# First MoE, layer one, as seven products over pairs of token blocks, with x operands streamed from DRAM

## The chip, the cores and the metric

The kernel runs on one core of one Trainium2 chip. The metric is device time in microseconds (us), from the start to the end of one execution. TensorE is PE in the profile, VectorE DVE, ScalarE ACT, GpSimd POOL; SP issues the DMAs.

## The reference, cut to what matters

Attention with pooled queries gives x (2304 tokens x 512). A first mixture of experts (MoE) with 8 experts follows, then a second, soft one. The change concerns the first:

```python
P = sinkhorn_like(x @ w_gate)                 # 2304 x 8
for e in range(8):
    h = np.maximum(x @ w1[e], 0.0)            # layer one: 2304x512 @ 512x1024
    out += P[:, e:e + 1] * (h @ w2[e])        # layer two: 2304x1024 @ 1024x512
```

## The kernel before

Every float32 product is made from three matmuls in the shorter type fp32r: each operand is held as a high half (ACT copies it) and a low half (DVE subtracts the high half from the original), and PE adds hi·hi, hi·lo and lo·hi in one PSUM bank. So each operand costs an ACT and a DVE operation, called a split below; its halves stand side by side in one tile.

The tokens form 9 blocks of 256. The names: `xa` is the output of attention, `xs` an x tile with both halves, `w` a tile of W1, `v` of W2, `g` a PSUM bank of layer one, `hr` the rectified result, `ht` a sum of quarters of h, `ho` a split of h, `y` a PSUM bank of layer two, `acc` the output's accumulator.

Attention comes first: score matmuls (L189), their maximum on DVE (L190), exponentials on ACT (L221), sums of these on POOL (L225, L227). It takes a table of hooks: work for the MoE that is put between its steps (one split of w, one of x, four loads).

Then follow the experts. For experts 0 to 6 `period(e, i, after)` writes one block's work in a fixed text order: the seven products (L583) of layer two of block i, mixed with four quarters (`g1`, L541 to L549) of layer one of the next block. Layer one of a quarter is 24 matmuls of 128x256 (4 rows of D by 2 columns of F by 3), 96 per block and 864 per expert. Layer two of these experts is already done in seven products over halves of tokens, F and D (`PRODUCTS`): `h_sum` makes s1 to s4 on DVE, `h_split` splits seven operands, each product is 12 matmuls, and an eighth is never made. `v_sum` and `v_split` do this for W2. Expert 7 has an order of its own, since the tail of the kernel is woven into it.

The order on each engine is that of the text: the tile framework gives waits but moves nothing. Around the products the text is filled up by `slot()` (the gate's steps and the first preparations) and by `at(name, ...)` (splits of the next expert's weights). x of all blocks is stored to DRAM once (`xd`, 1 MB a block with both halves) and loaded again for each block of every expert (`load_x`, three buffers). The last phase loads the second MoE's weights (`load_m2`) as buffers come free. All these DMAs are on SP's queue.

Of the kernel before, what the change touches and what calls it, by code (L numbers as in the profile page):

```python
# [8 lines left out]
F32 = mybir.dt.float32  # L9
# [348 lines left out]
def tile_attention__moe__softmoe(ctx, tc, q, k, v, w_gate, w1, w2, phi, m2_w1, m2_w2, out):  # L358
# [9 lines left out]
    stg_p = ctx.enter_context(tc.tile_pool(name="stg", bufs=4))  # L368
# [49 lines left out]
    ]  # L418

    def stage(e, p):  # L420
        t = stg_p.tile([128, 1024], F32, tag="stg", name="stg")
        if isinstance(p, tuple):
            src = w2[e][512 * p[0]:512 * p[0] + 512, 256 * p[1]:256 * p[1] + 256].rearrange("(c p) d -> p c d", p=128)
            nc.sync.dma_start(out=t.rearrange("p (c d) -> p c d", c=4), in_=src)
        elif p < 4:
            src = w1[e][:, 256 * p:256 * p + 256].rearrange("(k p) f -> p k f", p=128)
            nc.sync.dma_start(out=t.rearrange("p (k f) -> p k f", k=4), in_=src)
        else:
            src = w2[e][256 * (p - 4):256 * (p - 4) + 256].rearrange("(c p) d -> p c d", p=128)
            nc.sync.dma_start(out=t.rearrange("p (c d) -> p c d", c=2), in_=src)  # L430
        staged[e, p] = t

    def split_w(e, p, eng=None):
        t = staged.pop((e, p))
        if p > 3:
            u = wpools["m"].tile([128, 2, 1024], F32R, tag="v", name="v", bufs=7)
        elif (4 * e + p) % 5 == 0:
            u = wp_p.tile([128, 2, 1024], F32R, tag="wp", name="w", bufs=1)
        else:
            u = wpools["m"].tile([128, 2, 1024], F32R, tag="w", name="w", bufs=4)  # L440
        nc.scalar.copy(u[:, 0], t)
        (eng or nc.vector).tensor_tensor(out=u[:, 1], in0=t, in1=u[:, 0].bitcast(F32), op=ALU.subtract)  # L442
        pieces[e, p] = u

    V = {}


    def v_sum(e, k):
        q = [staged[e, x] for x in ((0, 0), (0, 1), (1, 0), (1, 1))]
        if k == 4 and e == 0:  # L450
            staged[e, "t4"] = stg_p.tile([128, 1024], F32, tag="stg", name="t4")
        elif k == 4:
            staged[e, "t4"] = q[2]
        dst, a, b = {1: (q[0], q[1], q[0]), 2: (q[0], q[3], q[0]), 3: (q[1], q[3], q[1]), 4: (staged.get((e, "t4")), q[2], q[0])}[k]
        nc.vector.tensor_tensor(out=dst, in0=a, in1=b, op=ALU.subtract)

    def v_split(e, j):
        src = staged[e, ((0, 0), (1, 0), (0, 0), (0, 0), (0, 1), (1, 1), "t4")[j]]
        u = V[e, j] = wpools["m"].tile([128, 2, 1024], F32R, tag="v", name="v", bufs=7)
        nc.scalar.copy(u[:, 0], src)  # L460
        nc.vector.tensor_tensor(out=u[:, 1], in0=src, in1=u[:, 0].bitcast(F32), op=ALU.subtract)


    X, Hh, acc, Xd = {}, {}, {}, {}

    def x_tile(v):
        pool, tag = (wpools["m"], "x") if v % 3 else (wp_p, "x0")
        X[v] = pool.tile([128, 2, 4, 256], F32R, tag=tag, name="xs", bufs=2 if v % 3 else 1)
        return X[v]

    def split_x(i):
        u = x_tile(i)
        src = xa[i].rearrange("p k n -> p (k n)")
        hi, lo = (u[:, z].rearrange("p k n -> p (k n)") for z in range(2))
        nc.scalar.copy(hi, src)
        nc.vector.tensor_tensor(out=lo, in0=src, in1=hi.bitcast(F32), op=ALU.subtract)
        if i:
            store_x(i)
# [35 lines left out]

    Ho = {}
# [4 lines left out]
    def h_sum(i, name):  # L520
# [7 lines left out]
        nc.vector.tensor_tensor(out=o, in0=a, in1=b, op=op)  # L528

    def h_split(i, j):  # L530
        x = PRODUCTS[j][0]
        src = Ho[i, x] if isinstance(x, str) else part(i, *x)
        o = Ho[i, j] = m_p.tile([128, 2, 4, 128], F32R, tag="ho", name="ho", bufs=4)
        nc.scalar.copy(o[:, 0], src)  # L534
        nc.vector.tensor_tensor(out=o[:, 1], in0=src, in1=o[:, 0].bitcast(F32), op=ALU.subtract)  # L535

    def g1(e, i, fp, mid=None):
        x = X[NBLK * e + i]  # L540
# [636 lines left out]
```

## Time and profile before

| | |
|---|---|
| median of 3 runs | 2209.32 us (2208.95 to 2210.77) |
| span of the profiled execution | 2207.6 us |
| PE busy | 2162.6 us (98%) |
| DVE busy | 1280.8 us (58%) |
| ACT busy | 852.7 us (39%) |
| POOL busy | 414.5 us (19%) |

The median is of other executions than the profiled one; 1.7 us lie between it and the span. Busy shares are averages over three stages: attention up to about 530 us, the first MoE with experts 0 to 6 and then expert 7, and the end. POOL works in attention alone.

### The profile page before, as it was taken

What the parts mean: (1) busy time and instruction counts of PE and PEld (TensorE: products, weight loads), DVE (VectorE), ACT (ScalarE), POOL (GpSimd) and SP (SyncE); (2) the same over time, 40 slices, a digit from 0 to 9 for tenths busy, and PEclk for the clock granted to TensorE, in tenths of its full rate; (3) what the DMA queues carried; (4) which work ended last, traced back from release to release, by engine and by line L of the source; (5) the groups of instructions that cost most, each with busy time, mean ns of one, the idle gap of its engine ahead of it and who ended that gap; (6) DMA issues with size and microseconds to landing.
All of it is one profiled execution on the core that took longest, in us unless ns stands there. A gap on an engine that the chain in (4) does not pass through costs nothing.

```text
span 2207.6 us, 40414 instructions
## 1 busy us (share of the span) xinstructions
PE 2162.6 (98%) x16789; PEld 1955.1 (89%) x16789; DVE 1280.8 (58%) x2391; ACT 852.7 (39%) x1779; POOL 414.5 (19%) x305
## 2 busy tenths in 40 slices
PE   7999999998999999999999999999999999999997
PEld 5777777766999999999999999999999999999863
DVE  5777777775565654665474456447445744633451
ACT  3555555554433432333243233324233432311232
POOL 5888878874000000000000000000000000000000
PEclk9999999999999999999999999999999999999998
DMA  7554565451122221212122121212112121566668
GB/s 171 142 119 114 129 137 122 108 152 45 58 77 87 77 87 39 96 58 77 58 87 85 41 96 59 77 49 96 67 59 87 68 77 49 186 257 221 224 228 277
DMA packets 125045, 239.66 MB, mean 109 GB/s; under 512 B 44096, under 2 KB 95808, under 8 KB 110144
## 3 DMA queue, kind: packets, MB, share of 16 engines
q1 hardware_dynamic: 124864, 237.08, 34.8%
q8 instruction: 133, 2.18, 0.4%
q14 instruction: 48, 0.39, 0.1%
HBM read 189.87 MB, written 14.16 MB: 92 GB/s over the span
## 4 chain that ended last, share of the span: by engine, by line
PE 95%; DVE 2%; DMA 1%; ACT 1%; POOL 1%; issue 0%; SPq 0%; ACTq 0%; DVEq 0%; POOLq 0%
PE y L583 29%; PE g L547 13%; PE g L549 12%; PE g L548 12%; PE se L218 7%; PE o L234 7%; PE S L189 4%; PE y L659 2%; PE y L660 1%; PE y L661 1%; PE f L1075 1%; DMA kd<-kp 1%; PE t L133 1%; PE t L244 1%; PE t L109 1%; PE t L202 1%
## 5 line engine op out<-in xcount | busy, mean ns | idle before, releaser
L583 PE MATMUL y<-v,ho 128*128 128x256 f32 x5292 | 678.1, 283 | 4.0 <-DVE ho L535 2.2
L583 PEld LDWEIGHTS y<-v,ho 128*128 128x128 f32 x5292 | 654.0, 192 | 4.3 <-DVE ho L535 2.4
L547 PE MATMUL g<-xs,w 128*128 128x256 f32 x2304 | 654.9, 284 | 0.0
L549 PE MATMUL g<-xs,w 128*128 128x256 f32 x2304 | 652.0, 283 | 1.0 <-DVE w L442 1.0
L548 PE MATMUL g<-xs,w 128*128 128x256 f32 x2304 | 651.9, 283 | 0.0
L547 PEld LDWEIGHTS g<-xs,w 128*128 128x128 f32 x2304 | 441.9, 192 | 5.4 <-issue 4.0
L548 PEld LDWEIGHTS g<-xs,w 128*128 128x128 f32 x2304 | 442.1, 192 | 1.0
L549 PEld LDWEIGHTS g<-xs,w 128*128 128x128 f32 x2304 | 442.0, 192 | 1.2 <-DVE w L442 1.2
L565 ACT ACTIVATE hr<-g 128x512 f32<-128x512 f32 x252 | 150.5, 597 | 731.1 <-PE g L549 729.2
L595 DVE SCALAR_TENSOR_TENSOR acc<-y,P,acc 128x256 f32<-128x256 f32 x378 | 181.0, 481 | 321.0 <-PE y L583 321.0
L227 POOL TENSOR_TENSOR acc<-acc,e 128x576 f32<-128x576 f32 x224 | 319.0, 1424 | 64.7 <-ACT e L221 54.5
L190 DVE TENSOR_REDUCE m<-S 128x1 f32<-128x384 f32 x432 | 230.5, 547 | 86.7 <-PE S L189 75.1
L763 POOL MEMSET HT<- 128x1024 f32 x2 | 1.9, 960 | 1385.9 <-ACT ho L534 1375.0
L221 ACT ACTIVATE e<-se 128x288 f32<-128x288 f32 x576 | 206.7, 411 | 88.1 <-PE se L218 84.9
L218 PE MATMUL se<-q,kd 128*128 128x288 f32 x1152 | 223.4, 311 | 2.1 <-ACT e L221 0.3
L218 PEld LDWEIGHTS se<-q,kd 128*128 128x128 f32 x1152 | 178.0, 190 | 17.0 <-ACT e L221 9.8
L528 DVE TENSOR_TENSOR ht<-hr 128x512 f32<-128x512 f32 x126 | 86.7, 688 | 177.8 <-ACT hr L565 177.7
L534 ACT CAST ho<-ht 128x512 fp32r<-128x512 f32 x252 | 149.8, 618 | 85.6 <-DVE ht L528 71.1
L234 PE MATMUL o<-e,vr 128*64 128x288 f32 x1152 | 171.5, 419 | 0.0
L535 DVE TENSOR_TENSOR ho<-ht,ho 128x512 fp32r<-128x512 f32 x252 | 166.7, 681 | 4.0 <-ACT ho L534 3.5
L189 PE MATMUL S<-kd,q 128*128 128x384 f32 x384 | 146.2, 385 | 5.1 <-DVE m L190 3.1
L535 DVE TENSOR_TENSOR ho<-hr,ho 128x512 fp32r<-128x512 f32 x189 | 129.6, 686 | 17.5 <-ACT ho L534 17.5
(170 smaller groups left out, 1793.0 us busy)
## 6 DMA issues: line engine op xcount, KB each, us to landing
xs<-xd SPq DMA_DIRECT2D x90, 1024.0 KB, 4.8
stg<-in_moe_w_dram SPq DMA_DIRECT2D x60, 512.0 KB, 5.7
kd<-kp SPq DMA_DIRECT2D x32, 576.0 KB, 6.4
m2w<-in_moe_w_dram SPq DMA_DIRECT2D x13, 1024.0 KB, 7.0
m2w<-in_moe_w_dram SPq DMA_DIRECT2D x24, 512.0 KB, 8.8
kr<-in_k_dram SPq DMA_DIRECT2D x32, 288.0 KB, 7.0
qr<-in_q_dram SPq DMA_DIRECT2D x16, 576.0 KB, 3.7
kd<-kp SPq DMA_DIRECT2D x32, 288.0 KB, 3.6
```

The costliest lines, as they stand in the source:

```text
L189: nc.tensor.matmul(ps, lhsT=w, rhs=r[:, 384 * n:384 * n + 384], start=True, stop=True)
L190: nc.vector.tensor_reduce(out=M_[ph][:, x, n:n + 1], in_=ps, axis=AX.X, op=ALU.max)
L218: nc.tensor.matmul(ps, lhsT=kd[:, z, 128 * c:128 * c + 128], rhs=y[:, h, g], start=z == 0, stop=z == 1)
L221: nc.scalar.activation(out=e[:, g], in_=ps, func=AF.Exp, scale=1.0 / 16)
L227: nc.gpsimd.tensor_tensor(out=acc_[ph], in0=acc_[ph], in1=e, op=ALU.add)
L234: nc.tensor.matmul(O_[ph][64 * g:64 * g + 64, :288], lhsT=raws["v"][pi][:, h, c, :], rhs=E_[ph, c][:, g], start=c == 0, stop=c == 8,)
L535: nc.vector.tensor_tensor(out=o[:, 1], in0=src, in1=o[:, 0].bitcast(F32), op=ALU.subtract)
L547: nc.tensor.matmul(o, lhsT=w[:, 0, kk, c], rhs=x[:, 0, kk], start=kk == 0, stop=False)
L548: nc.tensor.matmul(o, lhsT=w[:, 0, kk, c], rhs=x[:, 1, kk], start=False, stop=False)
L549: nc.tensor.matmul(o, lhsT=w[:, 1, kk, c], rhs=x[:, 0, kk], start=False, stop=kk == 3)
L583: nc.tensor.matmul(ps, lhsT=o[:, x, c], rhs=v[:, w, c], start=first and c + z == 0, stop=c + z == 5, skip_group_check=not first,)
L595: nc.vector.scalar_tensor_tensor(out=y, in0=ps, scalar=p, in1=y, op0=ALU.mult, op1=ALU.add)
```

## The change

Layer one of experts 0 to 6 is made in seven products too. The blocks are taken in four pairs (u = 0 to 3) and one single block (u = 4), in the order 0, 1, 4, 2, 3. D and F are halved, W1 is four quarters (11, 12, 21, 22), and the two blocks of a pair are the two columns of a 2x2 product. W1 is needed in seven forms: 11, 12, 22 and the sums S1 to S4. x is needed in seven operands per pair: B11, B21 and B22 (halves of blocks) and the sums T1 to T4. A `chunk(e, u, n, c)` is 12 matmuls: product n, half c of the 512 columns of F. A pair has 14 chunks, so 168 matmuls where two blocks had 192; the single block keeps 8 chunks, 96 matmuls.

Each operand of x is split once, 35 in all, stored in DRAM as 512 KB and loaded for every expert into three buffers. Preparing them is the larger part of what moves: the operands of two pairs and half of a third, three W1 sums with their splits and a fourth sum, and the four W2 sums (stored raw in DRAM) are now hooks in attention; 15 more steps are spread over expert 0. The sums of the next expert's weights, and s3 and s4 of h, go to POOL.

The result of product 0 (shared by four outputs) is copied by ACT into two PSUM banks, `seed0` and `seed1`, into which products 2, 3 and 4 then accumulate; ACT copies or rectifies what stands there between them. Products 5 and 6 stand in `g` banks and are added on DVE into `hr`. PSUM now has two `g` banks (before 3) and three of tag m (before 2), two of which are the seeds during these experts.

The core of the diff:

```diff
+    PAIR = [("11", "B11"), ("12", "B21"), ("S2", "T2"), ("S3", "T3"), ("22", "T4"), ("S1", "T1"), ("S4", "B22")]
+    ONE = [("11", "B11"), ("12", "B21"), ("S1", "B11"), ("22", "BD")]
...
+    def x_split(u, op, part):
+        t = stg_p.tile([128, 2, 512], F32R, tag="stg", name="xt")
+        nc.scalar.copy(t[:, 0], part)
+        nc.vector.tensor_tensor(out=t[:, 1], in0=part, in1=t[:, 0].bitcast(F32), op=ALU.subtract)
+        Xd[u, op] = dram_p.tile([128, 1024], F32, name=f"xd{u}{op}")
...
+    def load_x(n=1):
+        for _ in range(n):
+            if xseq:
+                key = xseq.pop(0)
+                t = Xt[key] = wp_p.tile([128, 2, 2, 256], F32R, tag="x", name="xs", bufs=3)
+                nc.sync.dma_start(out=t.rearrange("p z k n -> p (z k n)").bitcast(F32), in_=Xd[key[1:]])
...
+    for h, step, fs in ((-210, 8, prep(0)), (-134, 4, prep(1)), (-36, 8, X2[:4])):
+        for n, f in enumerate(fs):
+            hooks[h + step * n] = [f]
+            hooks[h + step * n + 2] = [store_x]
...
+        -92: lambda: w_split(0, "11"),
+        -88: lambda: w_sum(0, "S3"),
+        -80: lambda: w_split(0, "S3"),
+        -72: lambda: w_sum(0, "S1"),
+        -64: lambda: w_sum(0, "S2"),
+        -56: lambda: w_split(0, "S2"),
+        -48: lambda: w_split(0, "12"),
+        -40: lambda: w_sum(0, "S4"),
+        -24: lambda: load_x(3),
...
+        -276: lambda: v_store(1),
+        -266: lambda: v_store(3),
+        -256: lambda: v_store(2),
+        -246: lambda: v_store(4),
...
-    pg = ctx.enter_context(tc.tile_pool(name="pg", bufs=3, space=PSUM, reuse_waits="tile"))
+    pg = ctx.enter_context(tc.tile_pool(name="pg", bufs=2, space=PSUM, reuse_waits="tile"))
+    pm = ctx.enter_context(tc.tile_pool(name="pm", bufs=3, space=PSUM, reuse_waits="tile"))
...
+    def chunk(e, u, n, c):
+        one = u == 4
+        form, op = (ONE if one else PAIR)[n]
+        first = n in ((0, 2) if one else (0, 5))
+        if first:
+            G[c] = pg.tile([128, 512], F32, tag="g", name="g")
+        mid = not one and n in (2, 3, 4)
+        ps = seed[c] if mid else G[c]
...
+        if c == 1:
+            if one:
+                load_x((0, 0, 2, 1)[n])
+            else:
+                load_x()
...
+        elif n in (2, 3):
+            nc.scalar.copy(quad(B, n - 2, c, True), ps)
+        elif n == 4:
+            relu(quad(A, 1, c, True), ps)
         else:
...
+            o = quad(B, 6 - n, c)
+            nc.vector.tensor_tensor(out=o, in0=ps, in1=o, op=ALU.add)
+            relu(o, o)
...
+                    pos = merge(e, u, ch, "cppcppcppcpcccc", (pe_, i))
...
+            merge(e, u, ch, "cccccc", None)
+            r = bounds[e, u] = len(items) - 1
+            pos = merge(e, u, ch, "pccppcppcpp", (e, 2 * u))
...
+            for form, d in (("S3", -6), ("S1", -4), ("S2", 1), ("S4", 5)):
+                at(r + d, (w_sum, n, form, nc.gpsimd), **late)
...
+            for k, d in ((1, 16), (3, 18), (2, 23), (4, 25)):
+                at(r + d, (v_sum, n, k, nc.gpsimd), **late)
...
+    for j, f in enumerate([*prep(4), *X2[4:], *prep(3)]):
+        at(starts[0, 1] + 2 + 3 * j, (f,), **late)
+        at(starts[0, 1] + 4 + 3 * j, (store_x,), **late)
```

In the texts given to `merge`, c is a chunk and p a product of layer two.

PE, in a steady pair of the changed kernel: six chunks stand in a row on the seed banks, then products (L706) and chunks in `g` banks are mixed. A row with x12 is a chunk or a product.

```order
L706 MATMUL y_10278<-v_9476,ho_10357 128x256 x12
L661 MATMUL seed0_6742<-xs_10229,w_9071 128x256 x12
L661 MATMUL seed1_6760<-xs_10229,w_9071 128x256 x12
L661 MATMUL seed0_6742<-xs_10272,w_8809 128x256 x12
L661 MATMUL seed1_6760<-xs_10272,w_8809 128x256 x12
L661 MATMUL seed0_6742<-xs_10354,w_8855 128x256 x12
L661 MATMUL seed1_6760<-xs_10354,w_8855 128x256 x12
L706 MATMUL y_10505<-v_9114,ho_10471 128x256 x12
L661 MATMUL g_10533<-xs_10439,w_8941 128x256 x12
L661 MATMUL g_10548<-xs_10439,w_8941 128x256 x12
L706 MATMUL y_10565<-v_9196,ho_10527 128x256 x12
```

Before, a run of 24 single matmuls of L547 to L549 on one `g` bank stood between two products; the rows below are the first and the last ones around one such run.

```order
L583 MATMUL y_13752<-v_13280,ho_13659 128x256 x12
L583 MATMUL y_13639<-v_13446,ho_13705 128x256 x12
L547 MATMUL g_13785<-xs_13134,w_13077 128x256
L548 MATMUL g_13785<-xs_13134,w_13077 128x256
L549 MATMUL g_13785<-xs_13134,w_13077 128x256
```

What moved: chunks are half as long, take another x tile each time, and product 1 comes three pieces after the last seed chunk.

SP's queue behind the single block of an expert in the changed kernel; `xd4` is the single block's operand, `xd2` those of the next pair, PE_49 a wait for PE, DMAHW for the landing of an earlier DMA.

```order
L565 DMA xs_12091<-xd4BD_7333 128x1024 [waits DMAHW3_49,PE_49]
L565 DMA xs_12323<-xd2B11_5999 128x1024 [waits DMAHW5_49,PE_49]
L565 DMA xs_12325<-xd2B21_6177 128x1024 [waits DMAHW4_49,PE_49]
L565 DMA xs_12356<-xd2T2_7528 128x1024 [waits DMAHW6_49,PE_49]
L565 DMA xs_12397<-xd2T3_7392 128x1024 [waits DMAHW7_49,PE_49]
```

And PE there: the third form reads xs_11936, whose buffer the load of xs_12323 takes.

```order
L661 MATMUL g_12297<-xs_11936,w_11083 128x256 x12
L661 MATMUL g_12310<-xs_11936,w_11083 128x256 x12
L661 MATMUL g_12297<-xs_12091,w_11009 128x256 x12
L661 MATMUL g_12310<-xs_12091,w_11009 128x256 x12
L661 MATMUL g_12359<-xs_12323,w_10853 128x256 x12
```

Before, one load of a whole block stood on SP's queue for each block, three blocks ahead of its use:

```order
L486 DMA xs_11496<-xd4_7369 128x2048
L427 DMA stg_11618<-in_moe_w1_dram 128x4x256
L486 DMA xs_11732<-xd5_7634 128x2048
L427 DMA stg_11851<-in_moe_w1_dram 128x4x256
L486 DMA xs_11965<-xd6_7899 128x2048
```

What moved: a load now waits for a tile that PE releases two chunks before the loaded tile is used.

POOL at the change from one expert to the next, in the changed kernel: W1 sums (L452), W2 sums (L483) and s3, s4 of h (L628). Before, POOL's last row ahead of the tail was a sum of attention (L227), so nothing stood here, and these sums were DVE's.

```order
L452 TENSOR_TENSOR stg_10721<-stg_10721,stg_10717 128x1024
L628 TENSOR_TENSOR ht_11185<-hr_10897 128x512
L628 TENSOR_TENSOR ht_11187<-hr_10930,ht_11183 128x512
L483 TENSOR_TENSOR stg_10916<-stg_11065,stg_10916 128x1024
L483 TENSOR_TENSOR stg_11065<-stg_11121,stg_11065 128x1024
L483 TENSOR_TENSOR stg_10916<-stg_11121,stg_10916 128x1024
```

What moved: eight sums of 128x1024 per change of expert and two of 128x512 per block went from DVE to POOL.

## Rows read from the trace of the kernel before

**Rows 1.** The page: busy time of each engine, and the chain that ended last.
```profile
PE 2162.6 (98%) x16789; PEld 1955.1 (89%) x16789; DVE 1280.8 (58%) x2391; ACT 852.7 (39%) x1779; POOL 414.5 (19%) x305
...
PE 95%; DVE 2%; DMA 1%; ACT 1%; POOL 1%; issue 0%; SPq 0%; ACTq 0%; DVEq 0%; POOLq 0%
```

**Rows 2.** Windows: length, busy PE, PEld, DVE, ACT, POOL (count), clock, DMA share, GB/s.
```profile
200.00:400.00 200.00, 198.94 (x1321) 141.93 (x1321) 150.83 (x325) 115.25 (x312) 161.97 (x116) 1.00 0.53 122
540.00:550.00 10.00, 6.03 (x47) 5.19 (x46) 6.79 (x10) 4.37 (x7) 0.00 (x0) 0.93 0.25 105
550.00:560.00 10.00, 10.00 (x82) 8.53 (x82) 8.58 (x13) 6.62 (x11) 0.00 (x0) 0.90 0.11 41
1000.00:1200.00 200.00, 200.00 (x1669) 200.00 (x1669) 109.22 (x181) 69.38 (x113) 0.00 (x0) 1.00 0.20 69
2100.00:2207.00 107.00, 86.84 (x772) 52.45 (x771) 41.31 (x123) 29.88 (x100) 0.00 (x0) 0.92 0.81 261
```

**Rows 3.** Timeline of ACT in attention: start, length, engine, line, operation.
```profile
403.89 1.45 ACT L221 ACTIVATE e<-se 128x288 f32<-128x288 f32 x4
...
435.02 1.45 ACT L221 ACTIVATE e<-se 128x288 f32<-128x288 f32 x4
...
468.27 1.45 ACT L221 ACTIVATE e<-se 128x288 f32<-128x288 f32 x4
```

**Rows 4.** Timeline of DVE in attention: the two low halves of the hooks.
```profile
447.04 1.33 DVE L442 TENSOR_TENSOR w<-stg,w 128x1024 fp32r<-128x1024 f32 x1
...
461.93 1.70 DVE L476 TENSOR_TENSOR xs<-x,xs 128x1024 fp32r<-128x1024 f32 x1 [0.25 <-ACT xs L475]
```

**Rows 5.** Groups by form, 800 to 1800 us: busy, mean ns | idle before, releaser.
```profile
L595 DVE SCALAR_TENSOR_TENSOR acc<-y,P,acc 128x256 f32<-128x256 f32 x325 | 155.6, 481 | 276.6 <-PE y L583 276.6
L535 DVE TENSOR_TENSOR ho<-ht,ho 128x512 fp32r<-128x512 f32 x188 | 124.3, 681 | 0.0
L534 ACT CAST ho<-ht 128x512 fp32r<-128x512 f32 x188 | 111.5, 617 | 70.5 <-DVE ht L528 58.4 <-PE y L583 12.1
L565 ACT ACTIVATE hr<-g 128x512 f32<-128x512 f32 x185 | 110.5, 597 | 567.1 <-PE g L549 567.1
L528 DVE TENSOR_TENSOR ht<-hr 128x512 f32<-128x512 f32 x93 | 64.0, 688 | 132.6 <-ACT hr L565 132.6
L461 DVE TENSOR_TENSOR v<-stg,v 128x1024 fp32r<-128x1024 f32 x35 | 42.6, 1217 | 3.8 <-ACT v L460 3.8
```

**Rows 6.** Timeline of PE in attention: score matmuls with a wait behind the hooks.
```profile
452.60 0.45 PE L189 MATMUL S<-kd,q 128*128 128x384 f32 x1 [0.43 <-DVE m L190]
...
464.16 0.44 PE L189 MATMUL S<-kd,q 128*128 128x384 f32 x1 [1.09 <-DVE m L190]
```

**Rows 7.** Timeline of PE at the start of the MoE: rows with a wait.
```profile
528.47 0.71 PE L244 MATMUL t<-acc,ones 128*64 128x288 f32 x4 [1.15 <-POOL acc L227]
...
534.20 0.39 PE L549 MATMUL g<-xs,w 128*128 128x256 f32 x1 [0.95 <-DVE w L442]
...
546.19 0.50 PE L583 MATMUL y<-v,ho 128*128 128x256 f32 x2 [1.79 <-ACT ho L534]
548.87 2.50 PE L583 MATMUL y<-v,ho 128*128 128x256 f32 x10 [2.18 <-DVE ho L535]
```

**Rows 8.** The page's DMA issues: count, KB each, median us to landing.
```profile
xs<-xd SPq DMA_DIRECT2D x90, 1024.0 KB, 4.8
...
q<-q SPq DMA_DIRECT2D x16, 288.0 KB, 3.4
```

**Rows 9.** The page's costliest groups: POOL's sums in attention.
```profile
L227 POOL TENSOR_TENSOR acc<-acc,e 128x576 f32<-128x576 f32 x224 | 319.0, 1424 | 64.7 <-ACT e L221 54.5
```

**Rows 10.** Timeline of POOL beside the two hooks.
```profile
445.87 6.76 POOL L227 TENSOR_TENSOR acc<-acc,e 128x576 f32<-128x576 f32 x4 [0.66 <-ACT e L221]
...
461.14 3.76 POOL L227 TENSOR_TENSOR acc<-acc,e 128x576 f32<-128x576 f32 x2
```

**Rows 11.** The chain that ended last, at the tail; then SP's timeline there.
```profile
2180.73 8.73 DMA m2w<-in_moe_w_dram
...
2154.89 27.25 SPq L913 DMA_DIRECT2D m2w<-in_moe_w_dram  x20
```

More of the change, by code (lines that the diff above doesn't have):

```diff
@@ L464, in tile_attention__moe__softmoe @@
[L464 to L478, printed above, removed]
@@ new lines, in tile_attention__moe__softmoe @@
+    ORDER = [(0, 1, 4, 2, 3)] * (E - 1)
+    Xt = {}
+    xseq = [
+        (e, u, op) for e in range(E - 1) for u in ORDER[e]
+        for op in ([y for _, y in PAIR] if u < 4 else ["B11", "B21", "BD"])
+    ]
+    def load_x(n=1):
[4 more added lines that the diff above has]
+                nc.sync.dma_start(out=t.rearrange("p z k n -> p (z k n)").bitcast(F32), in_=Xd[key[1:]])
@@ L499, in tile_attention__moe__softmoe @@
+    with ExitStack() as actx:
+        attention(actx, nc, tc, q, k, v, xa, ident, ones, hooks)
     ctx.enter_context(tc.manual_schedule())
@@ L566, in g1 @@
-        if fp == 3 or e == E - 1:
-            load_x(NBLK * e + i + 3)
+            cols = slice(256 * c + 128 * f2, 256 * c + 128 * f2 + 128)
+            for kk in range(2):
+                for z, (a, b) in enumerate(((0, 0), (0, 1), (1, 0))):
+                    begin = first and f2 + kk + z == 0
+                    nc.tensor.matmul(
+                        o, lhsT=w[:, a, kk, cols], rhs=x[:, b, kk], start=begin, stop=kk == 1 and z == 2,
+                        skip_group_check=not first or f2 > 0,
+                    )
@@ new lines, in second, with merge @@
+    def second(e, i, pos, plan):
+        s0, s12, s1, *others = plan
+        at(s0, (h_split, i, 0))
+        at(s12, (h_sum, i, "s1"), (h_sum, i, "s2"))
+        at(s12, (h_sum, i, "s3", nc.gpsimd), (h_sum, i, "s4", nc.gpsimd))
+        at(s1, (h_split, i, 1))
+        for j, k in enumerate(others):
+            at(k, (h_split, i, 2 + j), late=0.5)
+        if e == 1:
+            at(pos[0] - 2, (scale0, i))
+    def merge(e, u, chunks, text, block):
+        pos = []
+        for c in text:
+            if c == "c":
+                item(chunk, e, u, *chunks.pop(0))
+            else:
+                pos.append(item(product, *block, len(pos)))
+        return pos
@@ new lines, in tile_attention__moe__softmoe @@
+    late = dict(late=True)
+    for k, form in ((1, "22"), (3, "S1"), (5, "S4")):
+        at(k, (w_split, 0, form), **late)
+    for k, j in ((4, 0), (6, 1), (7, 2), (9, 6), (11, 3), (13, 4), (15, 5)):
+        at(k, (v0_split, j), **late)
+    for j, f in enumerate([*prep(4), *X2[4:], *prep(3)]):
+        at(starts[0, 1] + 2 + 3 * j, (f,), **late)
+        at(starts[0, 1] + 4 + 3 * j, (store_x,), **late)
+    at(starts[1, 0], (const2,), late=True)
+    gate = gate_steps()
+    for n, f in enumerate(gate):
+        if f is not None:
+            at(5 + 2 * n if n < 18 else 8 + 2 * n, (f,), **late)
@@ L1017, in tile_attention__moe__softmoe @@
+    for f, after in items:
+        f()
+        for _, fs in sorted(after, key=lambda x: x[0]):
+            for g in fs:
+                g()
     steps = [tail2_steps(i) for i in range(NBLK)]
```

496 lines of the change are left out of this document (268 added, 228 removed).

## The prediction

> **What bounds the kernel now.** The page comes first: how busy each engine is, and who carries the chain that ended last. TensorE (PE) is busy for 98% of the span and carries 95% of that chain [rows 1]. So time is won by taking PE work away, and lost wherever PE is made to wait. Next come the windows. From 560 to 1800 us (the row of 1000 to 1200 stands for six alike) PE has no idle time at full clock: 1669 matmuls in 200 us, 0.1198 us each [rows 2]. In those stages VectorE (DVE) is busy 109 of 200 us, ScalarE (ACT) 69, and GpSimd (POOL) does nothing. In attention it is otherwise: DVE is at 151 and POOL at 162 of 200 us while PE is almost full too. The boundary between attention and the MoE is the only stage with plain holes: between 540 and 550 us PE is busy for 6.0 of 10 us [rows 2].
>
> **What the change removes.** In the program, layer one of experts 0 to 6 falls from 864 to 768 matmuls of 128x256 each: per pair of blocks 14 chunks x 12 = 168 in place of 192, for four pairs; the single block keeps 96. That is 7 x 96 = 672 matmuls, and at 0.1198 us **-80.5 us**. Two seeding matmuls of 512 columns come once: +0.5. Everything else is a question of how much of this PE gives back by waiting.
>
> **Attention.** 20 splits of x operands, 4 splits and 4 sums of W1 and 4 sums of W2 now lie between its steps. Counted with the sums inside the operands, DVE gets 28 operations of 128x512 and 12 of 128x1024, where before it had two of 128x1024. The trace shows what those two cost. ACT's group of four exponentials recurs at 403.89 and 435.02, a period of 31.13 us; the next period, which holds both splits, ends at 468.27, 33.24 us [rows 3]. So two wide operations cost **2.1 us**, 1.06 each. The way is seen in three views: the two subtractions took 1.33 and 1.70 us [rows 4] against 1.22 in the MoE [rows 5], POOL's sums beside them grew, and score matmuls then waited for DVE's maximum [rows 6]. Low bound: only the wide ones cost anything, 12 x 1.06 - 2.1 = +10. High bound: all 40 cost as much, 40 x 1.06 - 2.1 = +40. In proportion to width, with the 512-wide at half: 12 x 1.06 + 28 x 0.53 - 2.1 = +25. I take **+20**, a little below that, since PE's waits behind those two were for 1.09 and 0.43 us [rows 6], so part of a short operation fits into slack.
>
> **The start of the MoE.** Before, PE waits 1.15 + 0.95 + 1.79 + 2.18 = 6.1 us there [rows 7], and behind the last wait ten matmuls take 2.50 us, twice their time. The clock of 540 to 560 reads 0.93 and 0.90 [rows 2], so part of that stretch runs at the lower level, 1.2 GHz, after PE's idle time. The change keeps such holes: the raw W2 loads stand ahead of an x load, and the gate's steps now have one PSUM bank where they had two, so each waits for the copy of P, which stands on DVE behind wide subtractions of 1.22 us. From a gain of 2 us to a loss of 9 (seven more wide operations); I take **+3**.
>
> **Expert 0.** 15 more preparing steps are spread over its chunks. DVE idles 277 us in 1000 waiting for y alone [rows 5], so most is covered. 0 to +12 (each costs one 512-wide subtraction of 0.68); I take **+4**.
>
> **The stream of x.** 512 KB tiles in three buffers. Within pairs each load has at least two chunks with products between. At the end of the single block it does not: SP's load of the next pair's B11 waits until PE is done with the third form, and then only two chunks of 12 stand before its use, 24 x 0.1198 = 2.88 us. The trace has no DRAM load of 512 KB of this kind. 288 KB takes 3.4 us and 1024 KB 4.8 [rows 8]; in between, 3.8. PE waits 0.95 us, with 0.1 for issue 1.05; seven times, **+7.5**. Behind the waiting load stands that of B21 on SP's queue; its first use is a chunk and a product later, so it is not late too. Bounds 3.4 - 2.88 and 4.8 - 2.88: +3.6 to +13.4. (The Trainium skill, DMA: Bandwidth & Descriptors, "Anatomy of one DMA", has 2.0 us plus bytes at 436 GB/s for GpSimd's path, 3.2 us here; the term would be an estimated +2.3. No run here shows it.)
>
> **Steady pairs.** Between the last seed chunk and product 1 stand three pieces of PE work, 3 x 12 x 0.1198 = 4.3 us. In that time must run: the relu 0.60, sums s1 and s2 0.69 each, the split's halves 0.62 and 0.68 [rows 5], with 0.3 to start, 3.6 us. Slack 0.7 us: one 512-wide operation ahead fits, a 1024-wide one (1.2) does not. 0 to +5, I take **+2**. ACT's copies into the seed banks, DVE's four adds of a G bank to hr per pair and the two half loads per block of expert 7 I put at nothing: DVE (109 of 200 us) and ACT (69) cover the first two [rows 2], and expert 7's loads run three steps of 24 matmuls ahead; without that cover an add would cost its 0.68, 28 x 4 x 0.68 = 76 us in all.
>
> **The next expert's weights.** Six times, four sums for W1 and four for W2 of 128x1024 go to POOL, and DVE has 14 wide subtractions. POOL's 128x576 sum takes 1.42 us [rows 9]; a sum of 1024 columns then 2.53, an s3 or s4 of 512 columns 1.27. What do they do to DVE? [rows 10]: four sums beside the first split took 6.76 us where 4 x 1.42 = 5.69, so +1.07; two beside the second 3.76, +0.92. With what DVE lost (0.11 and 0.48) that is 1.2 and 1.4 us, the whole of the DVE operation's length: the two never ran at once. DVE in turn waited for no more than the rest of one POOL operation. (The Trainium skill, SBUF — State Buffer, "Who interferes with whom", says why: a DVE instruction with two SBUF inputs contends with a GpSimd one that reads SBUF, the port pair is held for a whole instruction, and the loser fully blocks. The rows agree.) In the text such places come twice per change of expert: s4 with two sums of the second half of u=3 (6.3 us of POOL) and two sums in the next first half (5.1 us), each between a lo-half and the product that needs it. If DVE had to wait for all of it, less one and a half (2.2) and one product (1.4) that PE has queued, PE loses 4.1 + 3.7 = 7.8 us per change, 47 in all. If it got in at once, nothing beyond 0.5, +3. If each DVE operation waits for half a sum (1.27) and two stand in a row at each place, 2.5 less 0.9 of slack, 1.6 x 2 x 6 = **+20**. I take that; the measured waits of 0.11 and 0.48 speak for no more.
>
> **The tail.** Its chain ends on weight loads: 27.25 us of SP's issues and 8.73 us of one load [rows 11]. One megabyte more is loaded before it; at 261 GB/s [rows 2] that is 3.8 us less, **-3.5**, if buffers are free as early; -6 to +3.
>
> **Sum.** -80.5 + 0.5 + 20 + 3 + 4 + 7.5 + 2 + 20 - 3.5 = -27. The profiled span is 2207.6 us, 1.7 below the median 2209.3; I carry the 1.7 over: 2207.6 - 27 + 1.7 = **2182 us**. A measurement tells 0.2%, 4.4 us, from no change.
>
> **The rivals.**
> *A, nearly all is won* (0.20). Splits in attention cost their low bound, transitions and expert 0 nothing, loads their low bound: -80 + 10 + 3 + 3.6 - 3.5 = -67, 2142 us; up to 2160. For it: DVE is at 109 of 200 us in the MoE. Against it: the period of 33.24.
> *B, the forecast* (0.50): 2160 to 2200.
> *C, DVE is the bound in attention* (0.16). All 40 operations cost 1.06 there and expert 0 loses its 12: -27 + 20 + 8 = about 0, 2209; from 2200 to 2214. For it: DVE and POOL both over 75% busy. Against: 28 of the 40 are half as wide.
> *D, slower: POOL's sums hold DVE* (0.14). Without its term the sum is -47. There are 48 such sums; from 47 / 48 = 1.0 us of PE lost per sum the saving is gone. Were each paid in full, 48 x 2.53 = 121, the time would be 2283; at half of that, 2222. For it: DVE and POOL excluded each other in the rows, and 126 sums s3 and s4 go to POOL too. Against: in the rows POOL lost more than DVE, and PE has queued work. The rule of the page named above, taken at its strongest, is this case.
> That the seven products are not fewer matmuls can't be: the program has 672 fewer.
>
> **How the numbers follow.** A and B are faster; of C's 0.16, 0.08 is faster, 0.07 the same, 0.01 slower; of D's 0.14, 0.02 faster, 0.01 same, 0.11 slower. Faster 0.80, same 0.08, slower 0.12. The range leaves out the lowest of A (0.07) and the greater part of D (0.11): 2146 to 2215. The likeliest case's own is 2160 to 2200.
>
> **What would show it.** PE's matmul count down by 670; 128x256 matmuls still 0.120 us apart in the MoE at clock 1.00. The four exponentials in attention more than 31.13 us apart where hooks lie, with score matmuls waiting for DVE. Seven waits of PE for an x load, each near 1 us, behind the single block. Waits of products for DVE around each change of expert, with POOL sums of about 2.5 us beside them. I am wrong if attention grows by over 40 us, if POOL's sums take much more than 2.5 us, or if waits appear in steady pairs, since 28 pairs times any wait is much.

## The result: slower by 1.1%, and the profile after

The changed kernel takes 2233.28 us (median of 4 runs, 2229.86 to 2238.5) against 2209.44 us of the kernel before on the same chip: a ratio of 1.0109, 95% interval 1.0095 to 1.0123. It was forecast at 2182 us, in a range of 2146 to 2215; the time lies above the range and on the other side of no change. The profiled execution has a span of 2232.6 us.

The page of the changed kernel (busy time of each engine; the chain that ended last), which answers to [rows 1]:

```profile
PE 2124.9 (95%) x16119; PEld 1899.6 (85%) x16119; DVE 1448.3 (65%) x2421; ACT 971.8 (44%) x1994; POOL 724.3 (32%) x479
...
PE 69%; DVE 20%; ACT 5%; issue 3%; DMA 1%; SPq 1%; POOL 1%; ACTq 0%; DVEq 0%; POOLq 0%
```

PE has 670 matmuls fewer, as the program says, and is busy for 37.7 us less. But the chain runs through DVE for 20% of the span (before, 2%). Two points of the program cut the span into stages: the last L244 of attention, and the start of the last big PE block of the end (x64). Here they are in PE's timeline, after first, then the second one before (the first one before is in [rows 7], 528.47):

```profile
557.30 0.71 PE L244 MATMUL t<-acc,ones 128*64 128x288 f32 x4 [1.15 <-POOL acc L227]
...
2178.26 8.71 PE L1224 MATMUL f<-m2w,misc 128*32 128x512 f32 x64 [0.38 <-DVE misc L990]
```

```profile
2149.65 8.65 PE L1075 MATMUL f<-m2w,misc 128*32 128x512 f32 x64 [0.38 <-DVE misc L891]
```

Attention ends 28.8 us later. From there to the last block it is 1621.0 us, before 1621.2: the first MoE gains nothing at all from its 672 missing matmuls, some 80 us. The end is 3.6 us shorter (2232.6 - 2178.26 = 54.3 against 2207.6 - 2149.65 = 58.0). 28.8 - 0.2 - 3.6 = 25.0, the whole difference of the spans.

**Where the MoE's 80 us went.** PE's timeline over one expert (1000 to 1200 us), rows with a wait:

```profile
1044.76 1.46 PE L706 MATMUL y<-v,ho 128*128 128x256 f32 x10 [0.18 <-DVE ho L635]
1076.68 3.11 PE L706 MATMUL y<-v,ho 128*128 128x256 f32 x24 [0.22 <-DVE acc L718]
1145.34 5.46 PE L706 MATMUL y<-v,ho 128*128 128x256 f32 x24 [3.61 <-DVE acc L718]
1166.83 1.67 PE L706 MATMUL y<-v,ho 128*128 128x256 f32 x12 [1.15 <-DVE acc L718]
1182.30 2.89 PE L706 MATMUL y<-v,ho 128*128 128x256 f32 x22 [0.60 <-DVE ho L635]
1192.22 1.78 PE L706 MATMUL y<-v,ho 128*128 128x256 f32 x13 [1.24 <-DVE acc L718]
1194.25 1.58 PE L706 MATMUL y<-v,ho 128*128 128x256 f32 x11 [0.25 <-DVE v L462]
```

The last of these rows comes again at 1388.98, and six of its kind span 804.04 to 1777.87: 194.8 us per expert. The matmuls alone need 1524 x 0.1198 = 182.6; the kernel before needed 1620 x 0.1198 = 194.1 and had no waits. So 12.2 us are lost per expert. The waits add up to 7.3 us, and all but 0.4 of it lies within 50 us, where the weights of the next expert are made. Part of the rest is the clock. Windows (length, busy PE, PEld, DVE, ACT, POOL, granted clock, DMA share, GB/s):

```profile
1140.00:1145.00 5.00, 1.72 (x15) 1.52 (x13) 4.50 (x3) 0.98 (x2) 3.63 (x2) 0.89 0.31 105
1145.00:1150.00 5.00, 4.67 (x22) 4.70 (x23) 2.86 (x6) 1.25 (x2) 1.28 (x1) 0.50 0.59 212
1150.00:1155.00 5.00, 5.00 (x41) 5.00 (x41) 2.96 (x6) 2.57 (x4) 0.00 (x0) 0.92 0.01 2
...
1000.00:1195.00 195.00, 187.73 (x1528) 185.97 (x1527) 125.63 (x175) 83.44 (x138) 45.99 (x26) 0.98 0.31 106
```

Behind the wait of 3.61 us the granted clock is 0.50, the lower level of 1.2 GHz, for about 5 us: 22 matmuls in 5 us, where 42 are usual. That costs some 2.4 us: the 24 matmuls there take 5.46 us, those of the row at 1076.68 3.11. Over the whole period PE is busy for 187.73 us with 1528 matmuls that need 183.1 at full clock, 4.7 us more. Most of the other 2.3 us lies around the waits, where the clock reads 1.00: each row behind a wait is some 0.24 us longer than 0.1198 us for each of its matmuls (12 in 1.67 us at 1166.83, 13 in 1.78 at 1192.22). 7.3 + 4.7 is the 12.

Two views show what DVE does ahead of the longest wait and in it: its timeline, and below it POOL's.

```profile
1137.07 1.61 DVE L635 TENSOR_TENSOR ho<-ht,ho 128x512 fp32r<-128x512 f32 x1
1138.61 0.68 DVE L689 TENSOR_TENSOR hr<-g,hr 128x512 f32<-128x512 f32 x1
1140.49 1.02 DVE L635 TENSOR_TENSOR ho<-ht,ho 128x512 fp32r<-128x512 f32 x1 [1.21 <-ACT ho L634]
1141.43 3.36 DVE L462 TENSOR_TENSOR w<-stg,w 128x1024 fp32r<-128x1024 f32 x1
1144.72 0.47 DVE L718 SCALAR_TENSOR_TENSOR acc<-y,P,acc 128x256 f32<-128x256 f32 x1
```

```profile
1136.84 1.30 POOL L628 TENSOR_TENSOR ht<-hr,ht 128x512 f32<-128x512 f32 x1 [9.42 <-DVE ho L635]
1138.10 5.62 POOL L452 TENSOR_TENSOR stg<-stg 128x1024 f32<-128x1024 f32 x2
```

DVE's subtraction at 1141.43 takes 3.36 us where 1.22 is usual, and the update of acc behind it, which PE waits for, comes 2.1 us late. Two splits ahead of it are stretched as well, by 0.93 us at 1137.07, beside s4, and by 0.34 at 1140.49 (0.68 is usual). Together the three are held for 3.4 us; PE waits for 3.61. The operation at 1138.61, which has one operand in PSUM, takes its usual 0.68 beside a running POOL sum. Only operations with two operands in SBUF are stretched. When sums of W2 are made, two splits of 0.68 us in a row are held, each by one of two sums:

```profile
1160.71 2.77 DVE L635 TENSOR_TENSOR ho<-ht,ho 128x512 fp32r<-128x512 f32 x1
...
1163.80 2.49 DVE L635 TENSOR_TENSOR ho<-hr,ho 128x512 fp32r<-128x512 f32 x1
```

```profile
1160.53 5.21 POOL L483 TENSOR_TENSOR stg<-stg 128x1024 f32<-128x1024 f32 x2 [1.82 <-DVE v L462]
```

Groups by form, 800 to 1800 us (mean ns), answering to [rows 5]:

```profile
L635 DVE TENSOR_TENSOR ho<-ht,ho 128x512 fp32r<-128x512 f32 x185 | 176.2, 955 | 77.1 <-ACT ho L634 75.1
L718 DVE SCALAR_TENSOR_TENSOR acc<-y,P,acc 128x256 f32<-128x256 f32 x326 | 156.4, 480 | 112.9 <-PE y L706 111.3
L462 DVE TENSOR_TENSOR w<-stg,w 128x1024 fp32r<-128x1024 f32 x35 | 63.5, 1815 | 4.0 <-ACT w L459 4.0
L452 POOL TENSOR_TENSOR stg<-stg 128x1024 f32<-128x1024 f32 x20 | 56.1, 2804 | 43.7 <-DVE w L462 42.9
```

0.955 against 0.681 us, 1.815 against 1.217; L718, with its operand in PSUM, is unchanged at 0.480.

### The profile page after: what moved, and what is told of

Its sections match the earlier page's. It is cut to its first block, busy times and chain, and to the rows that moved or that the text cites. A ratio compares the mean times of both kernels' runs of the same rounds, so it can differ in the third digit from the quotient of the medians.

```text
span 2232.6 us, 40083 instructions
## 1 busy us (share of the span) xinstructions
PE 2124.9 (95%) x16119; PEld 1899.6 (85%) x16119; DVE 1448.3 (65%) x2421; ACT 971.8 (44%) x1994; POOL 724.3 (32%) x479
## 4 chain that ended last, share of the span: by engine, by line
PE 69%; DVE 20%; ACT 5%; issue 3%; DMA 1%; SPq 1%; POOL 1%; ACTq 0%; DVEq 0%; POOLq 0%
PE y L706 20%; PE g L661 12%; PE seed L661 9%; PE o L234 5%; PE se L218 5%; DVE ho L635 5%; PE S L189 4%; ACT ho L634 2%; DVE v L462 2%; DVE acc L718 2%; DVE w L462 2%; DVE m L190 2%; DVE hr L689 1%; PE g L738 1%; PE g L739 1%
## 5 line engine op out<-in xcount | busy, mean ns | idle before, releaser
L706 PE MATMUL y<-v,ho 128*128 128x256 f32 x5292 | 704.5, 288 | 47.6 <-DVE acc L718 33.4
L706 PEld LDWEIGHTS y<-v,ho 128*128 128x128 f32 x5292 | 669.6, 195 | 61.2 <-issue 33.8
L661 PE MATMUL g<-xs,w 128*128 128x256 f32 x3360 | 442.7, 284 | 0.0
L661 PEld LDWEIGHTS g<-xs,w 128*128 128x128 f32 x3360 | 422.4, 193 | 1.4 <-issue 1.3
L227 POOL TENSOR_TENSOR acc<-acc,e 128x576 f32<-128x576 f32 x224 | 329.1, 1469 | 70.8 <-ACT e L221 60.2
L628 POOL TENSOR_TENSOR ht<-hr,ht 128x512 f32<-128x512 f32 x63 | 84.9, 1347 | 685.0 <-DVE ho L635 679.6
L635 DVE TENSOR_TENSOR ho<-ht,ho 128x512 fp32r<-128x512 f32 x252 | 232.6, 925 | 107.9 <-ACT ho L634 105.4
L718 DVE SCALAR_TENSOR_TENSOR acc<-y,P,acc 128x256 f32<-128x256 f32 x378 | 181.1, 480 | 133.1 <-PE y L706 131.2
L661 PE MATMUL seed<-xs,w 128*128 128x256 f32 x2016 | 247.7, 283 | 0.0
L661 PEld LDWEIGHTS seed<-xs,w 128*128 128x128 f32 x2016 | 244.2, 192 | 0.8 <-ACT v L459 0.4
L218 PEld LDWEIGHTS se<-q,kd 128*128 128x128 f32 x1152 | 179.1, 192 | 21.0 <-ACT e L221 14.5
L628 POOL TENSOR_TENSOR ht<-hr 128x512 f32<-128x512 f32 x63 | 84.2, 1337 | 300.5 <-ACT hr L670 300.5
L670 ACT ACTIVATE hr<-hr 128x512 f32<-128x512 f32 x112 | 69.9, 632 | 201.6 <-DVE hr L689 201.6
L189 PEld LDWEIGHTS S<-kd,q 128*128 128x128 f32 x384 | 74.3, 194 | 82.3 <-issue 31.9
L684 ACT COPY hr<-seed 128x512 f32<-128x512 f32 x112 | 65.8, 587 | 158.0 <-PE seed L661 157.9
```

What stands on the lines that cost most here:

```text
L189: nc.tensor.matmul(ps, lhsT=w, rhs=r[:, 384 * n:384 * n + 384], start=True, stop=True)
L218: nc.tensor.matmul(ps, lhsT=kd[:, z, 128 * c:128 * c + 128], rhs=y[:, h, g], start=z == 0, stop=z == 1)
L227: nc.gpsimd.tensor_tensor(out=acc_[ph], in0=acc_[ph], in1=e, op=ALU.add)
L628: (eng or nc.vector).tensor_tensor(out=o, in0=a, in1=b, op=op)
L635: nc.vector.tensor_tensor(out=o[:, 1], in0=p, in1=o[:, 0].bitcast(F32), op=ALU.subtract)
L661: nc.tensor.matmul(o, lhsT=w[:, a, kk, cols], rhs=x[:, b, kk], start=begin, stop=kk == 1 and z == 2, skip_group_check=not first or f2 > 0,)
```

## The experiments

All times are medians; ratios are to the kernel before on the same chip, with 95% intervals, and differences to the changed kernel are to its 2233.3. The changed kernel was not run again beside the experiments; the kernel before was, and took 2208.89 to 2209.96 us (medians).

### Who makes the sums: DVE or POOL

The weight sums of the next expert, on DVE:

```diff
-                at(r + d, (w_sum, n, form, nc.gpsimd), **late)
+                at(r + d, (w_sum, n, form), **late)
...
-                at(r + d, (v_sum, n, k, nc.gpsimd), **late)
+                at(r + d, (v_sum, n, k), **late)
```

> The eight sums of 128x1024 per change of expert go from POOL to DVE; s3 and s4 of h stay on POOL. Theory 'hold' (a running POOL sum of 2.8 us keeps DVE's operations with two SBUF inputs waiting, and everything behind them on DVE): the waits of 3.61 and 1.15 us at each change and the half-clock stretch behind the first go, DVE pays 8 x 1.14 = 9 us per change but no longer waits some 14; 6 changes x 6 to 9 us, 2180 to 2200 us. Theory 'load' (DVE simply has too much wide work at the change, whoever makes the sums): 9 us more of it per change lengthen the waits, 2245 to 2290 us.

2205.87 us, ratio 0.9989 (0.9980 to 0.9999): 27 us less than the changed kernel, although DVE now does more, but 6 us above the range of 'hold'. W1's subtractions are back at their length, and waits of PE over 800 to 1800 us fall from 36.4 us to 22.8. Groups by form there, then the waits (us in total, times, longest):

```profile
L462 DVE TENSOR_TENSOR w<-stg,w 128x1024 fp32r<-128x1024 f32 x35 | 42.7, 1220 | 5.3 <-ACT w L459 5.1
L452 DVE TENSOR_TENSOR stg<-stg 128x1024 f32<-128x1024 f32 x20 | 24.3, 1215 | 0.0
```

```profile
PE y L706 <- DVE acc L718: 17.5, 15, 2.4
PE y L706 <- DVE ho L635: 3.8, 16, 0.3
PE y L706 <- DVE v L462: 1.2, 5, 0.2
PE y L706 <- ACT ho L634: 0.3, 1, 0.3
```

s3 and s4 of h on DVE, weight sums left on POOL:

```diff
-        at(s12, (h_sum, i, "s3", nc.gpsimd), (h_sum, i, "s4", nc.gpsimd))
+        at(s12, (h_sum, i, "s3"))
+        at(others[1], (h_sum, i, "s4"), late=0.6)
```

> s3 and s4 of h go from POOL to DVE (s4 one split later in the text, since its buffer is free only then); the weight sums stay on POOL. 'Hold': the stretched product splits (0.955 and 0.866 us where 0.68 is usual) come back to 0.68 in steady pairs, but there PE waits only 0.2 us per expert, so little is won: 2222 to 2233. 'Load': two more operations of 0.61 us per block on DVE, 63 blocks, waits appear also in steady pairs, 2240 to 2265.

2228.01 us, ratio 1.0082 (1.0067 to 1.0097): at most a few us less, since the interval touches that of the changed kernel. The wait of 3.6 at a change is 3.87 us here, with the weight sums still on POOL.

Both on DVE:

> Both of the above: POOL idle in the MoE as before the change. 'Hold': 2175 to 2200, every DVE operation back at its usual length. 'Load': over 2260, waits behind each change longer than 3.6 us.

2206.16 us, ratio 0.9986 (0.9975 to 0.9997), as with the weight sums alone, and again above the range of 'hold'. So it is the wide sums that cost; the 126 short ones cost little that can be told. "Load" is refuted as what makes the changed kernel slower than these: all three versions give DVE more work than it, and none is slower. But DVE's load does cost something: with POOL idle, PE still waits for 2.36 us at the change, and 24 matmuls take 4.61 us behind that.

```profile
1139.30 4.61 PE L706 MATMUL y<-v,ho 128*128 128x256 f32 x24 [2.36 <-DVE acc L718]
```

An expert takes (1757.90 - 801.78) / 5 = 191.2 us here, by the row of a wait for v, and its matmuls need 182.6. So 8.6 us per change of expert are lost with no POOL work beside DVE's.

### Hold, or late data?

DVE's sums could also help only by being finished earlier. So POOL keeps them, at their places, each as four operations of 128x256 (and the same for W2's):

```diff
-        (eng or nc.vector).tensor_tensor(out=q[dst], in0=q[a], in1=q[b], op=op)
+        for c in range(0, 1024, 256) if eng else (0,):
+            z = slice(c, c + 256) if eng else slice(0, 1024)
+            (eng or nc.vector).tensor_tensor(out=q[dst][:, z], in0=q[a][:, z], in1=q[b][:, z], op=op)
```

> The weight sums stay on POOL and at their places, but each is four operations of 128x256. POOL has the same work or a little more. 'Hold by whole instruction': DVE waits for 0.7 us at a time in place of 2.8, most of what the move to DVE won comes back: 2208 to 2220. Rival 'late data' (the sums are simply finished later on POOL than on DVE, and the splits wait for them): no gain, 2232 to 2238.

2210.17 us, ratio 1.0005 (0.9995 to 1.0016): 23 us less, with POOL busy for longer (269.5 against 233.9 us in 800 to 1800). The same place in DVE's and POOL's timelines:

```profile
1130.45 1.75 DVE L464 TENSOR_TENSOR w<-stg,w 128x1024 fp32r<-128x1024 f32 x1
1132.12 0.47 DVE L722 SCALAR_TENSOR_TENSOR acc<-y,P,acc 128x256 f32<-128x256 f32 x1
```

```profile
1127.37 7.96 POOL L454 TENSOR_TENSOR stg<-stg 128x256 f32<-128x256 f32 x8
```

The subtraction takes 1.75 us in place of 3.36, beside POOL's work of the same sums, two of which take 7.96 us in place of 5.62. Late data is refuted; what counts for these 23 us is how long a single POOL instruction is. The Trainium skill, SBUF — State Buffer, "Who interferes with whom", states that a DVE instruction with two SBUF inputs contends with a GpSimd one that reads SBUF, and that the port pair they share is an exclusive lock. The traces agree: such operations were held for nearly a whole POOL sum (3.36 and 2.77 us), and those with a PSUM operand (0.68 us and 0.480) were not.

### Two mixes

W1's sums on DVE, W2's on POOL in four, s3 and s4 in two:

```diff
-                at(r + d, (w_sum, n, form, nc.gpsimd), **late)
+                at(r + d, (w_sum, n, form), **late)
...
+        for z in (slice(0, 2), slice(2, 4)) if eng else (slice(0, 4),):
+            (eng or nc.vector).tensor_tensor(out=o[:, z], in0=a[:, z], in1=b[:, z], op=op)
```

> W1's sums on DVE, W2's on POOL as four operations of 128x256, s3 and s4 of h on POOL as two of 128x256 each. 'Hold': POOL never holds DVE for longer than some 0.7 us and DVE has only four more wide operations per change, so the waits are below both mixes alone: 2198 to 2206. If what is left of the waits is DVE's own work at the change, no better than the two: 2206 to 2210.

2216.12 us, ratio 1.0029 (1.0020 to 1.0039): a miss, worse than either alone. Its longest wait of a change is 2.82 us, in the half where W1's sums are, and 1.12 and 0.61 us are waited in the half of W2's pieces. It looks as if DVE's own work fills the first half of a change and POOL's pieces the second, but why this mix is worse isn't shown: against the version with all sums in pieces two things differ, W1's sums and the cutting of s3 and s4, and the version with all sums on DVE is 10 us faster.

The other way round, W1's sums on POOL in four and W2's on DVE (the edit of the pieces above and `(v_sum, n, k)` on DVE):

> The other mix: W1's sums on POOL as four operations of 128x256, W2's on DVE; s3 and s4 of h on POOL, whole. In the runs so far, W1's sums in pieces left the first wait of a change at 1.73 us (on DVE 2.36 and 2.82), and W2's sums on DVE left 1.2 us in the next pair (in pieces 2.5 to 3). If the two halves are independent: some 3.3 us per change, 1 us less than with all on DVE, 2198 to 2204, faster than before by 0.2% or more. If the second half depends on how late the first ends: 2204 to 2209.

2195.97 us, ratio 0.9937 (0.9923 to 0.9950): faster than the kernel before by 0.6%, the best of all here and faster than either expectation. PE's timeline over one change, rows with a wait:

```profile
1128.69 3.10 PE L710 MATMUL y<-v,ho 128*128 128x256 f32 x24 [1.72 <-DVE acc L722]
1170.40 1.79 PE L710 MATMUL y<-v,ho 128*128 128x256 f32 x13 [0.91 <-DVE acc L722]
1172.43 1.57 PE L710 MATMUL y<-v,ho 128*128 128x256 f32 x11 [0.24 <-DVE v L464]
```

2.9 us at the change in place of 6.9, and no stretch at half clock behind the first wait (24 products' matmuls in 3.10 us, not 5.46). An expert takes (1736.27 - 794.53) / 5 = 188.3 us by the row of v, 6.4 less than in the changed kernel. Why this mix is the better one of the two stays open.

### What attention's growth is made of

Three parts of the work between attention's steps are left out in turn. (Of W1, four sums and four splits stand there; two of the splits are of a sum, not three, as the section on the change has it.) The x splits there (the 20 operands are stored unsplit and so are wrong):

```diff
     def x_split(u, op, part):
+        if u < 2 or (u == 2 and op in ("B11", "B21", "B12", "B22")):
+            Xd[u, op] = dram_p.tile([128, 1024], F32, name=f"xd{u}{op}")
+            for z in range(2):
+                stores.append(lambda z=z: nc.sync.dma_start(out=Xd[u, op][:, 512 * z:512 * z + 512], in_=part))
+            return
```

> The 20 splits of x operands among attention's steps are left out (ACT's copy and DVE's subtraction; the raw operand is stored twice instead, so these x operands are wrong); sums, W1 and W2 work and all else stay. Theory 'DVE bound in attention': 20 of 40 DVE operations are gone and attention shrinks by 10 to 16 us of its 28.8, to about 2219. Rival 'stores': the growth comes from the stores and loads on SP's queue, which stay (20 DMAs more even): no change, 2230 to 2236.

2228.51 us, ratio 1.0089 (1.0074 to 1.0104): 4.8 us less, half of what was expected.

The 8 sums of 128x512 of pairs 0 and 1:

```diff
+                    if u < 2:
+                        B[n] = B[a]
+                        continue
                     B[n] = t[:, 512 * z:512 * z + 512]
                     nc.vector.tensor_tensor(out=B[n], in0=B[a], in1=B[b], op=op)
```

> The 8 sums of 128x512 (T1 to T4 of pairs 0 and 1) among attention's steps are left out (the raw operand is split in place of the sum, so these operands are wrong); all 20 splits and stores stay. Theory 'burst': a hook with two sums and a split stands on DVE for 2 to 3 us in a row, ACT's copy for the split waits for the sum with exponentials queued behind it, and PE loses more there than at a lone split: 6 to 10 us less, 2223 to 2227. Rival 'width': only the 12 operations of 128x1024 cost anything: under 2 us, 2231 to 2234.

2223.8 us, ratio 1.0065 (1.0051 to 1.0079): 9.5 us less, twice what 20 splits cost.

The 8 sums of 128x1024 of expert 0's weights (`w_sum` and `v_sum` do nothing where e is 0):

> The 8 sums of 128x1024 (4 of W1, 4 of W2, for expert 0) among attention's steps are left out, so expert 0's weights are wrong; the splits, stores and loads stay, and all later experts too. 'Each operation at the price of the rows' (1.06 us per wide operation): 8.5 us less, about 2225. 'Burst' (a lone operation is mostly covered): 2 to 4 us less, 2229 to 2231.

2223.31 us, ratio 1.0063 (1.0047 to 1.0078): 10.0 us less, 1.25 each, somewhat over the 1.06 of the rows. By the last L244 of the profiled executions it is less: attention ends at 550.82, 547.84 and 550.67 us in these three versions, so 6.5, 9.5 and 6.6 us earlier than in the changed kernel, 0.8 for each of the wide sums. Versions that share their attention differ by 8 us in its end, so all these prices are rough.

All three parts at once:

> All 20 splits of x, the 8 sums of x and the 8 wide sums are left out among attention's steps (results wrong); what stays are the 4 splits of W1, the stores (20 of them doubled) and all loads. If DVE's and ACT's operations make the growth of 28.8 us, attention ends within 5 us of its end before (528.5) and the time is 2206 to 2212. Rival 'queue' (stores and loads on SP's queue delay attention's own loads): attention still ends 10 us or more later than before, over 2215.

2206.59 us, ratio 0.9986 (0.9977 to 0.9995): 26.7 us less; the three alone add up to 24.3. Attention ends at 533.09, 4.6 us later than before, with two wide subtractions more than before and all stores and loads in place:

```profile
533.09 0.71 PE L244 MATMUL t<-acc,ones 128*64 128x288 f32 x4 [1.12 <-POOL acc L227]
```

So most of the growth, 24.2 of 28.8 us by attention's end, is made by the operations, not by the DMAs. What the other 4.6 are isn't told apart.

Is it that two sums stand in a row with a split behind them? The changed kernel has such places: ACT's copy waits for DVE's sum, and the exponentials behind it wait too. Rows of ACT, DVE and PE there, in that order:

```profile
354.89 0.62 ACT L519 CAST xt<-xs 128x512 fp32r<-128x512 f32 x1 [3.42 <-DVE xs L540]
```

```profile
353.20 1.65 DVE L540 TENSOR_TENSOR xs<-xs,x 128x512 f32<-128x512 f32 x1
```

```profile
355.87 0.85 PE L218 MATMUL se<-q,kd 128*128 128x288 f32 x2 [2.13 <-ACT e L221]
```

Each sum was then made a step of its own:

```diff
-    for h, step, fs in ((-210, 8, prep(0)), (-134, 4, prep(1)), (-36, 8, X2[:4])):
+    for h, step, fs in ((-210, 5, prep(0, True)), (-134, 2.7, prep(1, True)), (-36, 8, X2[:4])):
...
+                half(0, "T3", "B22", "B12", ALU.subtract), half(1, "T1", "B12", "B11", ALU.subtract),
+                one("T3"), one("T1"),
+                half(0, "T2", "T3", "B11", ALU.add), half(1, "T4", "B21", "T2", ALU.subtract),
+                one("T2"), one("T4"),
```

> The same work as the changed kernel, but each of the 8 sums in attention is a step of its own, five or two to three steps from the next, so no hook puts more than one operation on DVE. 'Burst': 4 to 8 us less, 2225 to 2229. Rival 'amount' (each operation costs what it costs wherever it stands): 2231 to 2235.

2230.21 us, ratio 1.0094 (1.0079 to 1.0109): 3 us less, which the intervals do not tell from no change (the end of attention differs by more between profiles of versions that share it: 552.4 us with the pieces on POOL, 560.3 with all sums on DVE). And on top of the weight sums on DVE:

> Weight sums on DVE and attention's sums apart, together: if the two gains add, 2206 less 4 to 8 us, 2198 to 2202, which is faster than the kernel before (2209.4) by over 0.2%. If the hooks' amount decides, 2206.

2207.12 us, ratio 0.9986 (0.9977 to 0.9995), nothing beyond the 2205.87 without it. "Burst" is not borne out as the main cause. It isn't a clean test, though: sums apart bring the steps of pair 1 closer together. Why a sum of 128x512 cost 1.2 us and a split of the same width 0.24 stays open; leaving the sums out also spares the buffer that two of them share, and no run separates the two.

## Why the prediction was wrong, by its steps

**Removed matmuls.** Right: 670 fewer in the trace, 0.1198 us each where nothing waits.

**The next expert's weights: the step that failed.** The mechanism was named and its rows were read rightly (POOL and DVE exclude each other), and the upper bound of 47 us was worked out; then +20 was taken (its product, 1.6 x 2 x 6, is 19.2), and the slower end given to rival D with 0.14. It measured 12.2 us per change in five changes, 73 us for six if the first costs as much, or 1.5 us for each of 48 sums, past the 1.0 from which D decides. Two things were wrong. First, the price of the holds. I took half a sum per DVE operation, two operations at each of two places, less 0.9 us of slack, from two rows where DVE had waited 0.11 and 0.48 us. In those rows a single wide DVE operation met POOL's sums each time. Here sums and DVE operations stand ready on both queues, and they take turns, so that a DVE operation can wait for nearly a whole sum: at 1140.49 the first waits 0.34 us for the rest of the first sum, at 1141.43 the second waits 2.1 us for the second sum. PE waited at five places of a change, not at two, for 6.9 us in all. For six changes that is 41 us, close to the 47 of the upper bound and far from 20. Secondly, no term of this step held what follows a wait. The wait of 3.61 us brought half the pace behind it, some 2.4 us per expert or 14 us in all, although [rows 7] showed the same thing (ten matmuls in 2.50 us behind a wait of 2.18), and the starts behind the waits most of another 2.3 us per expert.

How much of the 73 us the holds make by themselves isn't shown, since no run leaves the sums out at the change. What is shown: shorter POOL instructions alone take off 23 us, and with the sums on DVE and POOL idle 8.6 us per change are lost as well, to DVE's own work.

**Attention.** 28.8 us, +20 taken, bounds of 10 to 40: the mechanism was right, the size too small. The way that was named, score matmuls waiting for DVE's maximum, is the largest wait of PE (us in total, times, longest; the changed kernel from 60 to 557 us, then the one before from 60 to 526):

```profile
PE S L189 <- DVE m L190: 15.1, 24, 1.6
```

```profile
PE S L189 <- DVE m L190: 1.8, 3, 1.1
```

PE's windows of this stage hold the same number of matmuls after and before:

```profile
57.00:557.00 500.00, 476.83 (x3081) 334.11 (x3079) 388.59 (x785) 282.90 (x754) 392.20 (x271) 0.99 0.56 141
```

```profile
57.00:528.00 471.00, 466.19 (x3081) 330.11 (x3078) 350.21 (x748) 271.47 (x733) 382.09 (x271) 1.00 0.51 122
```

Idle time grew by 18.4 us, from 4.8 to 23.2, and the same matmuls kept PE busy for 10.6 us more; part of that is the clock, which reads down to 0.77 in 350 to 360. By the experiments, roughly: the wide sums cost 0.8 to 1.25 where 1.06 was taken, 20 lone splits 0.24 to 0.33 rather than 0.53, the narrow sums 1.2 rather than 0.53. So only the narrow sums cost clearly more than forecast.

**The stream of x.** Taken at +7.5; it is 0. I had read the order wrongly: the load of B11 behind the single block takes the buffer of the second form, not, as the section on the change says, that of the third. SP issues it when the second form's last chunk ends (1056.34), and it is needed at 1063.3, behind four chunks. SP's row, PE's row of six chunks, and the page's row of such a load (median us to landing):

```profile
1056.34 4.64 SPq L565 DMA_DIRECT2D xs<-xd2B  x2
```

```profile
1057.58 8.80 PE L661 MATMUL g<-xs,w 128*128 128x256 f32 x72
```

```profile
xs<-xd2B SPq DMA_DIRECT2D x37, 512.0 KB, 3.3
```

3.3 us of landing fit into 7.0; the estimate of 3.8 was 0.5 too long besides.

**Start of the MoE and expert 0.** +3 and +4 were taken. What is left of the MoE's 79.8 lost us beside the 73 is 6.7: the sum fits, though the two terms were not measured apart and the first change was not either.

**Steady pairs.** +2 taken, 0.4 us per expert measured (0.18 and 0.22), 3 in all, which the 12.2 hold already: right.

**The tail.** -3.5 taken, -3.6 measured: right in size. The DMAs moved 14.5 MB there (266 GB/s over 54.3 us) where they had moved 16.1 (278 over 58.0), which bears the reason out, but no run tests it.

With 73 for 20, 29 for 20 and 0 for 7.5, the sum of the prediction would have been 2182 + 53 + 9 - 7.5, some 2236; 2233 was measured.

## What to carry to other kernels

A sum that is moved to POOL isn't free for DVE. Where DVE's operations have two operands in SBUF, count a whole POOL instruction as their wait at each place where both queues are full, and cut POOL's work into short instructions or keep it on DVE: six changes of expert cost 73 us with whole sums on POOL, 52 us, 6 x 8.6, with all on DVE, and 34 us, 6 x (188.3 - 182.6), with W1's in pieces and W2's on DVE. Which sums to cut and which to move had to be tried: the other mix took 20 us more. And a saving on PE has to be weighed at the few places where work is dense, with the half clock that followed the longest waits here, not at the mean occupation of DVE, which was 65%.

## What the hardware showed unexpectedly

When both queues are full, DVE and POOL alternate, instruction by instruction; sixteen POOL pieces of 256 columns in a row took 15.09 us in the first of the two mixes, 0.94 each, with DVE operations in between. And after 3.61 us without work PE's granted clock was at 0.50 for the next 5 us, while behind the wait of 1.15 us it reads 1.00 (1165 to 1170, PE busy for 3.85 us). The same wait comes back with every expert, and at 1534.93 it cost less: 24 matmuls took 4.23 us, and the clock reads 0.66 in 1535 to 1540.
